# Layer 2 of a fused attention and two-layer kernel: five token tiles in place of six

## The chip, the cores and the metric

The kernel runs on one core of one Trainium2 chip. The time is that of the device for one execution, in microseconds (us); the median of three runs is quoted. PE is TensorE (PEld its weight loads), DVE is VectorE, ACT is ScalarE, POOL is GpSimd, and SP is the engine that issues nearly all of the DMAs.

## The reference, cut to what matters

Attention over q, k and v of 4 batches, 8 heads, 576 positions and 64 elements a head (heads 0 to 3 look back 32 positions, heads 4 to 7 at every 32nd position before), and then two layers on 2304 tokens of width 512, with 2048 hidden columns in each.

```python
scores = np.where(masks[None, :, :, :], scale * np.matmul(q, k.transpose(0, 1, 3, 2)), -1000000000.0)
attn = np.exp(scores - np.max(scores, axis=-1, keepdims=True))
attn_out = np.matmul(attn / (np.sum(attn, axis=-1, keepdims=True) + 1e-09), v)
x = attn_out.transpose(0, 2, 1, 3).reshape(B * S, H * D)
h = np.maximum(x @ w_in, 0.0)
x = h * h @ w_out                                     # layer 1
h = x @ w_in2
g = np.maximum(h, 0.0) + alpha * np.minimum(h, 0.0)
return g @ w_out2                                     # layer 2
```

## The kernel before

The tokens are ordered so that layer 1 runs over seven tiles: three of 256 tokens (the first three blocks of 64 of every batch) and four of 384. `COLS` and `OFFS` hold their widths and starts. Layer 2 runs over six tiles of 384 tokens (`NTILE = 6`, `T` = 384).

The program is a list of steps. A step is one tile and one of 16 blocks `f` of 128 hidden columns. `emit_h` multiplies the block's 128 columns of `w_in` with the tile's x, on PE, into the PSUM bank `ps_h`: 4 chunks of the width 512, and 3 matmuls a chunk, since every operand is held as a high part and a low part (`xh`, `xl`, and the two halves of a weight slot `w{f}`) and three of the four products are taken. That is 12 matmuls, each over all the columns of the tile. `emit_g` applies the activation: for layer 2 two ACT instructions out of PSUM (`g` and `u`), one on DVE that joins them with alpha, and one ACT copy that makes the high part `gh`; `emit_gl` makes the low part `gl` on DVE one step later. `emit_y` multiplies with `w_out` into the PSUM banks `ps_y0` to `ps_y3`. In layer 1 the output is kept with its 512 columns on the partitions: 4 banks, 12 matmuls over the columns of the tile. In layer 2 the tokens are on the partitions: one bank for 128 tokens (`NSUB` = 3 of them in a tile), 3 matmuls a bank, each over 512 columns of `w_out`. On PE a step n therefore reads: the h part of step n+1, then the y part of step n, first the products with `gh` and then those with `gl`. After the last block of a tile `evac` copies the banks to SBUF and stores them: of layer 1 into a buffer `y1` in DRAM, of layer 2 into the output. `load_x2` and `split_x2` fetch layer 2's x from `y1` and split it.

Layer 1's x is written by the attention part, in buffers that `x_tile` hands out. The strided heads (class `Strided`) are worked out on DVE alone: keys and values are loaded by `load_kv` into the pool tag `kv`, and read by `score_mul` (L450) and `value_mul` (L491). The weights arrive as raw 64-bit words (`load_w`, L148, two DMAs of 512 KB for a block) and are turned into high and low parts by `convert_a` to `convert_d`, on ACT (L159, L162, L185) and DVE (L171, L172, L175, L191), between the other work: those of layer 1 during the first two tiles, those of layer 2 during the last tile of layer 1 and the first of layer 2.

The order on SP is the order in which the code issues (`manual_schedule`); so is ACT's from step 48 on. PE, DVE and, before step 48, ACT are ordered by the scheduler of the tile framework. A DMA on SP that waits for a buffer holds back all DMAs behind it.

Of the kernel before, what the change touches and what calls it, by code (L numbers as in the profile page):

```python
# [7 lines left out]
F32 = mybir.dt.float32  # L8
F32R = mybir.dt.float32r
# [7 lines left out]
P = 128  # L17
D = 64
# [1 line left out]
NEG = -1.0e30  # L20
EPS = 1e-9
SCALE = 1.0 / float(D) ** 0.5
NTILE = 6


TILES = [[(b, i) for b in range(4)] for i in range(3)] + [[(b, i) for i in range(3, 9)] for b in range(4)]
COLS = [D * len(blocks) for blocks in TILES]
OFFS = [sum(COLS[:t]) for t in range(len(TILES))]
# [42 lines left out]
def attn_moe_moe2(  # L71
# [37 lines left out]
    nc = tc.nc  # L109
    NT, DM = out.shape  # L110
    NF = w_in1.shape[0]
    NC = DM // P
    T = NT // NTILE
    NSUB = T // P

    cpool = ctx.enter_context(tc.tile_pool(name="const", bufs=1))
    wpool = ctx.enter_context(tc.tile_pool(name="w", bufs=1))
# [79 lines left out]

    def x_tile(t):
        if t not in x_sb:
            kw = {"bufs": 1} if t == 2 else {}  # L200
            x_sb[t] = tuple(
                xpool.tile([P, NC, COLS[t]], F32R, tag=nm[:2] if t != 2 else nm, name=f"{nm}{t}", **kw)
                for nm in ("xh_c", "xl_c")
            )
        return x_sb[t]


# [196 lines left out]
    class Strided:  # L404
# [15 lines left out]
        def load_kv(self, kind):  # L420

            b, e = self.b0, self.b0 + self.nb
            if kind == "k":
                t = spool.tile([P, self.nb, self.a1, D], F32, tag="kv", name="kv", bufs=3)
                src = ks[b:e, :, 0:self.a1, :].rearrange("b p a d -> p b a d")
            else:
                t = spool.tile([P, self.nb, D, self.a1], F32, tag="kv", name="kv", bufs=3)
                src = (vs1 if self.t == 2 else vs)[b:e].rearrange("b p d a -> p b d a")
            nc.sync.dma_start(out=t, in_=src)
            setattr(self, kind, t)  # L430
# [117 lines left out]
    steps = [(0, t, f) for t, f in FIRST]  # L548
    steps += [(0, t, f) for t in range(2, NL1) for f in range(NF)]
    SECOND = len(steps)  # L550
    steps += [(1, t, f) for t in range(NTILE) for f in range(NF)]
    g_sb, y_ps, ybank, hs = {}, {}, {}, {}
    x2, x2raw, y1 = {}, {}, {}

    def cols_of(n):
        return COLS[steps[n][1]] if n < SECOND else T

    def emit_h(n):
        l, t, f = steps[n]
# [11 lines left out]
    def emit_g(n):  # L571
        l, t, f = steps[n]
        m = cols_of(n)
        h = hs.pop(n)[:, 0:m]
        g = gpool.tile([P, T], F32, tag="g", name="g")[:, 0:m]
        gh = gpool.tile([P, T], F32R, tag="gh", name="gh")[:, 0:m]
        if l == 0:
            nc.scalar.activation(out=g, in_=h, func=AF.Relu)  # L578
            nc.scalar.activation(out=gh, in_=g, func=AF.Square)  # L579
            nc.scalar.activation(out=g, in_=g, func=AF.Square)  # L580
        else:
            u = spool.tile([P, T], F32, tag="pr", name="u", bufs=2)
# [16 lines left out]
    def emit_y(n):  # L599
        l, t, f = steps[n]  # L600
        gh, gl = g_sb.pop(n)
        w = wslot[l, f]
        no = NC if l == 0 else NSUB
        if f == 0:
            for o in range(no):
                if (l, t) != (0, 1):
                    ybank[o] = psum(f"y{o}")
                first = COLS[0] if (l, t) == (0, 1) else 0
                y_ps[l, t, o] = ybank[o][:, first:first + (cols_of(n) if l == 0 else DM)]
        order = [(part, o) for part in range(2) for o in range(no)]  # L610
# [15 lines left out]

    def evac(t, layer):
        no = NC if layer == 0 else NSUB
        cols = COLS[t] if layer == 0 else DM
        if layer == 0:  # L630
            y1[t] = dpool.tile([P, NC, cols], F32, tag=f"y1_{t}", name=f"y1_{t}")
        tags = (("so", 2, 1), ("wt", 2, 2)) if layer == 0 else (("so", 1, 1), ("sq", 1, 1), ("wt", 1, 2))
        if layer == 0 and t < 2:
            tags = (("wt", 2, 2),) * 2
        evs = []
        for tag, per, bufs in tags:
            ev = spool.tile([P, per, cols], F32, tag=tag, name="ev", bufs=bufs)
            evs += [ev[:, i, :] for i in range(per)]
        for o in range(no):
            ev = evs[o]  # L640
            y = y_ps.pop((layer, t, o))
            if layer == 1 and t == NTILE - 1 and o > 0:

                rows, half = slice(t * T + o * P, t * T + (o + 1) * P), DM // 2
                nc.vector.tensor_copy(ev[:, 0:half], y[:, 0:half])
                nc.sync.dma_start(out=out[rows, 0:half], in_=ev[:, 0:half])
                nc.scalar.activation(out=ev[:, half:], in_=y[:, half:], func=AF.Copy)
                nc.scalar.dma_start(out=out[rows, half:], in_=ev[:, half:])
                continue
# [89 lines left out]
    def plan():  # L739
        at(loads, 2 * NF, load_alpha)  # L740
        at(fill, 2 * NF + 4, negate_alpha)
        for t in range(2, NL1):
            base = (t - 1) * NF if t > 2 else 0
            for j, (u, p) in enumerate([(u, p) for u in range(2) for p in range(2)]):
                put_unit(base + UNITS_AT.get(t, (0, 3, 6, 9))[j], Unit(t, p, u), 3)
            first, last = STRIDED_AT.get(t, (0, 14))
            put_strided(base + first, base + last, t)
        put_kv_loads()
        for f in range(len(EARLY), NF):
            if f >= len(LOAD_AFTER):  # L750
# [213 lines left out]
```

## Time and profile before

| | |
|---|---|
| median of three runs | 889.06 us |
| the three runs | 888.34, 889.06, 896.01 us |
| the profiled execution, first to last instruction (its span) | 887.5 us |
| the profiled execution's own time | not recorded apart from its span |
| PE busy, share of the span | 866.4 us, 98% |
| DVE, ACT busy | 554.1 us, 453.0 us |

The median lies 1.6 us above the span: that is taken for what lies around the span. A busy share is a mean over stages: DVE is busy 62% of the whole, in layer 2 much less, in the first tiles nearly all the time. PE's matmuls overlap, so that a row's length is longer than the distance to the next; the distance between the starts of two rows is what a matmul costs.

### The profile page before, as it was taken

To read this page: it belongs to the slowest core of one execution; us is meant where nothing else is said; L and a number is where in the kernel's file an instruction comes from. 1 tells how busy PE (TensorE), PEld (TensorE's weight loads), DVE (VectorE), ACT (ScalarE), POOL (GpSimd) and SP (SyncE) were. 2 spreads that over 40 slices of the span, in tenths; PEclk is the share of its full clock that TensorE was granted. 3 is DMA by queue.
4 is the path that set the end of the run, shared out by engine and by line. 5 is a ranking of instruction groups with operands and counts; after the bars stand their busy time and mean duration, and the time that the engine had idled before them with its cause. 6 is when DMAs were issued, how large, how long until landed. Compare 5 with 4: busy or idle time off the path is not lost.

```text
span 887.5 us, 13794 instructions
## 1 busy us (share of the span) xinstructions
PE 866.4 (98%) x5448; PEld 814.4 (92%) x5448; DVE 554.1 (62%) x878; ACT 453.0 (51%) x1064; POOL 1.5 (0%) x10
## 2 busy tenths in 40 slices
PE   6799999999999999999999999999999999999997
PEld 5689999999999999999999999999999998999996
DVE  5899999996869788793687983233233233233222
ACT  5789756555445545454676663344344334334333
POOL 0000000000000000000000000000000000000000
PEclk9999999999999999999999999999999999999999
DMA  9990304221012212101777101001001001000001
GB/s 285 381 357 14 125 11 113 62 92 55 23 52 75 72 52 74 49 8 46 269 277 248 55 10 55 9 10 50 13 10 44 20 10 37 27 9 35 2 1 37
DMA packets 33825, 70.34 MB, mean 79 GB/s; under 512 B 5728, under 2 KB 18144, under 8 KB 33760
## 3 DMA queue, kind: packets, MB, share of 16 engines
q1 hardware_dynamic: 33472, 69.20, 23.0%
q8 instruction: 43, 0.70, 0.3%
q10 hardware_dynamic: 288, 0.26, 0.1%
q14 instruction: 22, 0.18, 0.1%
HBM read 60.01 MB, written 9.44 MB: 78 GB/s over the span
## 4 chain that ended last, share of the span: by engine, by line
PE 92%; DMA 5%; ACT 2%; DVE 1%; issue 0%; SPq 0%; ACTq 0%; DVEq 0%
PE ps_h L566 44%; PE ps_y L622 44%; DMA wraw<-in_w1o_dram 2%; DMA att_w<-in_q_dram 2%; PE ps_s L245 1%; PE ps_o L299 1%; DMA wraw<-in_w1i_dram 1%; PE ps_pt L289 1%; ACT wraw L159 0%; ACT att_w L267 0%; DVE g L585 0%; ACT ev L651 0%; DVE w L191 0%; DVE wt L172 0%; ACT wraw L162 0%
## 5 line engine op out<-in xcount | busy, mean ns | idle before, releaser
L566 PE MATMUL ps_h<-xh_c,w 128*128 128x384 f32 (+1 forms) x896 | 220.3, 314 | 3.2 <-DVE w L191 1.3
L566 PE MATMUL ps_h<-xh,w 128*128 128x384 f32 x768 | 212.5, 337 | 0.2 <-ACT u L584 0.2
L585 DVE SCALAR_TENSOR_TENSOR g<-u,nalpha,g 128x384 f32<-128x384 f32 x96 | 59.3, 618 | 192.1 <-ACT u L584 192.1
L594 DVE TENSOR_TENSOR gl<-g,gh 128x384 fp32r<-128x384 f32 (+1 forms) x208 | 109.2, 525 | 102.5 <-ACT g L580 52.4
L566 PEld LDWEIGHTS ps_h<-xh_c,w 128*128 128x128 f32 x896 | 156.9, 189 | 4.9 <-ACT w L185 1.6
L622 PE MATMUL ps_y<-gh,w 128*128 128x384 f32 (+1 forms) x896 | 158.3, 318 | 1.4 <-ACT gh L579 1.4
L622 PE MATMUL ps_y<-w,gh 128*128 128x512 f32 x576 | 149.3, 394 | 0.1
L566 PEld LDWEIGHTS ps_h<-xh,w 128*128 128x128 f32 x768 | 140.4, 188 | 4.8 <-ACT u L584 0.6
L622 PEld LDWEIGHTS ps_y<-gh,w 128*128 128x128 f32 x896 | 137.9, 189 | 2.8 <-ACT gh L579 1.6
L566 PE MATMUL ps_h<-xl_c,w 128*128 128x384 f32 (+1 forms) x448 | 139.9, 312 | 0.0
L583 ACT ACTIVATE g<-ps_h 128x384 f32<-128x384 f32 x96 | 47.2, 492 | 165.3 <-PE ps_h L566 165.2
L566 PE MATMUL ps_h<-xl,w 128*128 128x384 f32 x384 | 128.9, 336 | 0.0
L578 ACT ACTIVATE g<-ps_h 128x384 f32<-128x384 f32 (+1 forms) x112 | 49.6, 443 | 143.3 <-PE ps_h L566 141.8
L622 PEld LDWEIGHTS ps_y<-w,gh 128*128 128x128 f32 x576 | 106.5, 188 | 17.3 <-ACT gh L588 0.6
L588 ACT ACTIVATE gh<-g 128x384 fp32r<-128x384 f32 x96 | 50.5, 526 | 72.5 <-DVE g L585 72.5
L622 PE MATMUL ps_y<-gl,w 128*128 128x384 f32 (+1 forms) x448 | 86.1, 313 | 0.0
L566 PEld LDWEIGHTS ps_h<-xl_c,w 128*128 128x128 f32 x448 | 84.8, 189 | 0.1
L622 PE MATMUL ps_y<-w,gl 128*128 128x512 f32 x288 | 82.3, 392 | 0.0
L566 PEld LDWEIGHTS ps_h<-xl,w 128*128 128x128 f32 x384 | 72.1, 188 | 4.0
L622 PEld LDWEIGHTS ps_y<-gl,w 128*128 128x128 f32 x448 | 71.8, 189 | 0.4
L622 PEld LDWEIGHTS ps_y<-w,gl 128*128 128x128 f32 x288 | 54.1, 188 | 12.6
L580 ACT ACTIVATE g<-g 128x384 f32<-128x384 f32 (+1 forms) x112 | 53.6, 479 | 2.8
(100 smaller groups left out, 842.0 us busy)
## 6 DMA issues: line engine op xcount, KB each, us to landing
wraw<-in_w1i_dram SPq DMA_DIRECT2D x16, 512.0 KB, 8.9
wraw<-in_w1o_dram SPq DMA_DIRECT2D x16, 512.0 KB, 9.1
wraw<-in_w2i_dram SPq DMA_DIRECT2D x16, 512.0 KB, 3.7
wraw<-in_w2o_dram SPq DMA_DIRECT2D x16, 512.0 KB, 4.7
qk<-in_qk_dram SPq DMA_DIRECT2D x16, 336.0 KB, 3.9
out_dram<-ev SPq DMA_DIRECT2D x16, 256.0 KB, 2.3
y<-ev SPq DMA_DIRECT2D x16, 192.0 KB, 2.1
x2raw<-y SPq DMA_DIRECT2D x16, 192.0 KB, 3.2
```

Source lines behind the costliest of these rows:

```text
L245: nc.tensor.matmul(s, self.qk[:, j, 0:P], self.qk[:, j, P:], start=True, stop=True)
L289: nc.tensor.transpose(self.pt_ps[0:96, P * j:P * j + P], self.e[:, j, :], ident)
L299: nc.tensor.matmul(self.o[64 * h:64 * h + 64, 64 * j:64 * j + 64], self.v[:, j, D * h:D * h + D], self.pt[:, P * j + 64 * h:P * j + 64 * h ...
L566: nc.tensor.matmul(h[:, 0:b.shape[2]], a, b[:, c, :], start=(c == 0 and i == 0), stop=(c == NC - 1 and i == 2))
L578: nc.scalar.activation(out=g, in_=h, func=AF.Relu)
L580: nc.scalar.activation(out=g, in_=g, func=AF.Square)
L583: nc.scalar.activation(out=g, in_=h, func=AF.Relu)
L585: nc.vector.scalar_tensor_tensor(out=g, in0=u, scalar=nalpha[:, f:f + 1], in1=g, op0=ALU.mult, op1=ALU.add)
L588: nc.scalar.activation(out=gh, in_=g, func=AF.Copy)
L594: nc.vector.tensor_tensor(out=gl, in0=g, in1=gh.bitcast(F32), op=ALU.subtract)
L622: nc.tensor.matmul(y, a, b, start=(f == 0 and i == 0 and (l, t) != (0, 1)), stop=(f == NF - 1 and i == 2), skip_group_check=(l == 0 and t ...
```

## The change

Layer 2 runs over five tiles, three of 512 tokens and two of 384 (`WIDTHS`, `STARTS`); its buffers are as wide as the widest. A tile of 512 uses all four y banks, and `evac` has four buffers for it. The first two tiles of layer 1 share one buffer for x, of 512 columns, each its half; the third tile of layer 1 (256 columns), which had a buffer of its own, now takes the second of the two buffers. The pool tag `kv` has two buffers in place of three, and `put_kv_loads` looks two uses back.

```diff
-NTILE = 6
+WIDTHS = (512, 512, 512, 384, 384)
+STARTS = [sum(WIDTHS[:t]) for t in range(len(WIDTHS))]
...
-    T = NT // NTILE
-    NSUB = T // P
+    T = max(WIDTHS)
+    assert sum(WIDTHS) == NT
...
-            kw = {"bufs": 1} if t == 2 else {}
-            x_sb[t] = tuple(
-                xpool.tile([P, NC, COLS[t]], F32R, tag=nm[:2] if t != 2 else nm, name=f"{nm}{t}", **kw)
+            ts = (0, 1) if t < 2 else (t,)
+            whole = [
+                xpool.tile([P, NC, sum(COLS[u] for u in ts)], F32R, tag=nm[:2], name=f"{nm}{t}")
                 for nm in ("xh_c", "xl_c")
-            )
+            ]
+            for u in ts:
+                a = OFFS[u] - OFFS[ts[0]]
+                x_sb[u] = tuple(x[:, :, a:a + COLS[u]] for x in whole)
...
-                t = spool.tile([P, self.nb, self.a1, D], F32, tag="kv", name="kv", bufs=3)
+                t = spool.tile([P, self.nb, self.a1, D], F32, tag="kv", name="kv", bufs=2)
...
-        no = NC if l == 0 else NSUB
+        no = NC if l == 0 else WIDTHS[t] // P
...
-        tags = (("so", 2, 1), ("wt", 2, 2)) if layer == 0 else (("so", 1, 1), ("sq", 1, 1), ("wt", 1, 2))
+        tags = (("so", 2, 1), ("wt", 2, 2)) if layer == 0 else (("so", 1, 1), ("sq", 1, 1), ("wt", 1, 2), ("wt", 1, 2))
...
-        r = spool.tile([P, T], F32, tag="kv", name="x2raw", bufs=3)
+        r = spool.tile([P, T], F32, tag="kv", name="x2raw", bufs=2)[:, 0:WIDTHS[t]]
...
-            if i >= 3:
-                n = max(n, kv_uses[i - 3][0][1] + 1)
+            if i >= 2:
+                n = max(n, kv_uses[i - 2][0][1] + 1)
```

The change adds five lines to the file, so that a line of the changed kernel lies one to five lower than before.

The first place is the first step of layer 2. PE before, from the y part of the first block to the first of the next h part (`w1_0` is layer 2's block 0, `xh2_0` the x of its first tile):

```order
L622 MATMUL ps_y0_5623<-w1_0_5122,gh_5563 128x512 [waits Activation_49]
L622 MATMUL ps_y0_5623<-w1_0_5122,gh_5563 128x512
L622 MATMUL ps_y1_5624<-w1_0_5122,gh_5563 128x512 [waits Activation_49]
L622 MATMUL ps_y1_5624<-w1_0_5122,gh_5563 128x512
L622 MATMUL ps_y2_5625<-w1_0_5122,gh_5563 128x512 [waits Activation_49]
L622 MATMUL ps_y2_5625<-w1_0_5122,gh_5563 128x512
L622 MATMUL ps_y0_5623<-w1_0_5122,gl_5595 128x512 [waits DVE_49]
L622 MATMUL ps_y1_5624<-w1_0_5122,gl_5595 128x512
L622 MATMUL ps_y2_5625<-w1_0_5122,gl_5595 128x512
L566 MATMUL ps_h_5639<-xh2_0_5206,w1_2_5250 128x384 [waits Activation_49]
```

PE now:

```order
L626 MATMUL ps_y0_5621<-w1_0_5120,gh_5561 128x512 [waits Activation_49]
L626 MATMUL ps_y0_5621<-w1_0_5120,gh_5561 128x512
L626 MATMUL ps_y1_5622<-w1_0_5120,gh_5561 128x512 [waits Activation_49]
L626 MATMUL ps_y1_5622<-w1_0_5120,gh_5561 128x512
L626 MATMUL ps_y2_5623<-w1_0_5120,gh_5561 128x512 [waits Activation_49]
L626 MATMUL ps_y2_5623<-w1_0_5120,gh_5561 128x512
L626 MATMUL ps_y3_5624<-w1_0_5120,gh_5561 128x512 [waits Activation_49]
L626 MATMUL ps_y3_5624<-w1_0_5120,gh_5561 128x512
L626 MATMUL ps_y0_5621<-w1_0_5120,gl_5593 128x512 [waits DVE_49]
L626 MATMUL ps_y1_5622<-w1_0_5120,gl_5593 128x512
L626 MATMUL ps_y2_5623<-w1_0_5120,gl_5593 128x512
L626 MATMUL ps_y3_5624<-w1_0_5120,gl_5593 128x512
```

A fourth bank is added to the y part, and the matmuls of the h part (the row behind these) go over 512 columns in place of 384. DVE at the same place, before (`wraw_5499` and `wraw_5540` are the raw weights of blocks 13 and 14, `wt_5612` the work buffer of block 8):

```order
L171 TENSOR_SCALAR wraw_5499<-wraw_5499 128x1024 [waits DMAHW1_49,DMAHW0_49]
L585 SCALAR_TENSOR_TENSOR g_5562<-u_5564,nalpha_80,g_5562 128x384 [waits DVE_49,Activation_49]
L594 TENSOR_TENSOR gl_5595<-g_5562,gh_5563 128x384 [waits PE_49,Activation_49]
L172 SCALAR_TENSOR_TENSOR wt_5612<-wraw_5286 128x1024
L171 TENSOR_SCALAR wraw_5540<-wraw_5540 128x1024 [waits DMAHW3_49,DMAHW2_49]
L175 SCALAR_TENSOR_TENSOR wt_5612<-wraw_5286,wt_5612 128x1024 [waits DVE_49]
L585 SCALAR_TENSOR_TENSOR g_5616<-u_5618,nalpha_80,g_5616 128x384 [waits Activation_49]
```

DVE now:

```order
L172 TENSOR_SCALAR wraw_5497<-wraw_5497 128x1024 [waits DMAHW1_49,DMAHW0_49]
L589 SCALAR_TENSOR_TENSOR g_5560<-u_5562,nalpha_80,g_5560 128x512 [waits DVE_49,Activation_49]
L172 TENSOR_SCALAR wraw_5538<-wraw_5538 128x1024 [waits DMAHW3_49,DMAHW2_49,PE_49]
L598 TENSOR_TENSOR gl_5593<-g_5560,gh_5561 128x512 [waits Activation_49]
L173 SCALAR_TENSOR_TENSOR wt_5610<-wraw_5284 128x1024
L176 SCALAR_TENSOR_TENSOR wt_5610<-wraw_5284,wt_5610 128x1024 [waits DVE_49]
L589 SCALAR_TENSOR_TENSOR g_5614<-u_5616,nalpha_80,g_5614 128x512 [waits Activation_49]
```

The first instruction on the weights of block 14, which waits for their DMA, has moved ahead of the `gl` of layer 2's first step.

The second place is in the first two tiles. The queue of SP before (`kv_961` and `kv_1191` are the keys and the values of the second strided group, `wraw_1193` the weights of layer 1's block 14):

```order
L429 DMA kv_961<-in_ks_dram 128x2x384 [waits DMAHW0_49]
L415 DMA sq_1000<-in_qs_dram 128x2x128 [waits DMAHW1_49,DVE_49]
L148 DMA wraw_1002<-in_w1i_dram 128x1024 [waits DMAHW2_49]
L148 DMA wraw_1002<-in_w1o_dram 128x1024 [waits DMAHW3_49]
L230 DMA qk_1047<-in_q2_dram 128x448 [waits DMAHW4_49]
L238 DMA v_1049<-in_v2_dram 96x256 [waits DMAHW5_49]
L148 DMA wraw_1096<-in_w1i_dram 128x1024 [waits DMAHW6_49,PE_49,Activation_49]
L148 DMA wraw_1096<-in_w1o_dram 128x1024 [waits DMAHW7_49]
L429 DMA kv_1191<-in_vs1_dram 128x2x384 [waits DMAHW0_49]
L148 DMA wraw_1193<-in_w1i_dram 128x1024 [waits DMAHW1_49]
L148 DMA wraw_1193<-in_w1o_dram 128x1024 [waits DMAHW2_49]
L230 DMA qk_1244<-in_q2_dram 128x448 [waits DMAHW3_49,PE_49]
```

SP now:

```order
L433 DMA kv_959<-in_ks_dram 128x2x384 [waits DMAHW0_49,DVE_49]
L419 DMA sq_998<-in_qs_dram 128x2x128 [waits DMAHW1_49]
L149 DMA wraw_1000<-in_w1i_dram 128x1024 [waits DMAHW2_49]
L149 DMA wraw_1000<-in_w1o_dram 128x1024 [waits DMAHW3_49]
L234 DMA qk_1045<-in_q2_dram 128x448 [waits DMAHW4_49]
L242 DMA v_1047<-in_v2_dram 96x256 [waits DMAHW5_49]
L149 DMA wraw_1094<-in_w1i_dram 128x1024 [waits DMAHW6_49,PE_49,Activation_49]
L149 DMA wraw_1094<-in_w1o_dram 128x1024 [waits DMAHW7_49]
L433 DMA kv_1189<-in_vs1_dram 128x2x384 [waits DMAHW0_49,DVE_49]
L149 DMA wraw_1191<-in_w1i_dram 128x1024 [waits DMAHW1_49]
L149 DMA wraw_1191<-in_w1o_dram 128x1024 [waits DMAHW2_49]
L234 DMA qk_1242<-in_q2_dram 128x448 [waits DMAHW3_49,PE_49]
```

The order is the same. The keys now wait for DVE, as the load of the strided queries right behind them did before for the same reads, and the values wait for DVE too: for its last `value_mul` on the first group's values, whose buffer they take. ACT where the weights of block 14 are first used, before (`g_1077` and `gh_1078` belong to block 6 of the second tile):

```order
L185 ACTIVATE w0_9_1055<-wt_1020 128x2x512 [waits DVE_49]
L159 ACTIVATE wraw_1193<-wraw_1193 128x1024 [waits DMAHW2_49,DMAHW1_49]
L267 ACTIVATE e_1031,stat_1032<-e_1031,stat_1032 128x96 [waits DVE_49]
L578 ACTIVATE g_1077<-ps_h_1059 128x256 [waits PE_49]
L267 ACTIVATE e_1031,stat_1032<-e_1031,stat_1032 128x96
L579 ACTIVATE gh_1078<-g_1077 128x256 [waits Activation_49]
L516 ACTIVATE xh_c2_1131<-ot_1072 128x128 [waits DVE_49]
L580 ACTIVATE g_1077<-g_1077 128x256 [waits Activation_49]
L516 ACTIVATE xh_c2_1131<-ot_1074 128x128 [waits DVE_49]
L162 ACTIVATE wraw_1193<-wraw_1193 128x1024
L578 ACTIVATE g_1126<-ps_h_1101 128x256 [waits PE_49]
L579 ACTIVATE gh_1127<-g_1126 128x256 [waits Activation_49]
```

ACT now:

```order
L186 ACTIVATE w0_9_1053<-wt_1018 128x2x512 [waits DVE_49]
L271 ACTIVATE e_1029,stat_1030<-e_1029,stat_1030 128x96 [waits DVE_49]
L271 ACTIVATE e_1029,stat_1030<-e_1029,stat_1030 128x96
L520 ACTIVATE xh_c2_1129<-ot_1070 128x128 [waits DVE_49]
L520 ACTIVATE xh_c2_1129<-ot_1072 128x128 [waits DVE_49]
L582 ACTIVATE g_1075<-ps_h_1057 128x256 [waits PE_49]
L160 ACTIVATE wraw_1191<-wraw_1191 128x1024 [waits DMAHW2_49,DMAHW1_49]
L583 ACTIVATE gh_1076<-g_1075 128x256 [waits Activation_49]
L163 ACTIVATE wraw_1191<-wraw_1191 128x1024
L584 ACTIVATE g_1075<-g_1075 128x256 [waits Activation_49]
L582 ACTIVATE g_1124<-ps_h_1099 128x256 [waits PE_49]
L583 ACTIVATE gh_1125<-g_1124 128x256 [waits Activation_49]
```

The first instruction on block 14's weights, which waits for their two DMAs, now stands behind `g` and ahead of `gh` of block 6.

## Rows read from the trace of the kernel before

**Rows 1.** The page: busy tenths and granted clock in 40 slices; chain by engine.

```profile
PE   6799999999999999999999999999999999999997
...
PEclk9999999999999999999999999999999999999999
...
PE 92%; DMA 5%; ACT 2%; DVE 1%; issue 0%; SPq 0%; ACTq 0%; DVEq 0%
```

**Rows 2.** Busy time by stretch: us, PE, PEld, DVE, ACT, POOL, clock, DMA share.

```profile
640.00:720.00 80.00, 80.00 (x403) 72.45 (x402) 25.31 (x44) 30.09 (x66) 0.00 (x0) 1.00 0.07 23
```

**Rows 3.** Timeline of PE, layer 1, 256 columns: start us, us, what.

```profile
137.11 1.12 PE L622 MATMUL ps_y<-gh,w 128*128 128x256 f32 x8
...
138.55 0.28 PE L566 MATMUL ps_h<-xh_c,w 128*128 128x256 f32 x1
```

**Rows 4.** Timeline of PE, layer 1, 384 columns.

```profile
335.63 1.55 PE L622 MATMUL ps_y<-gh,w 128*128 128x384 f32 x8
...
337.71 0.33 PE L566 MATMUL ps_h<-xh_c,w 128*128 128x384 f32 x1
```

**Rows 5.** Timeline of one step of layer 2.

```profile
700.07 0.33 PE L566 MATMUL ps_h<-xh,w 128*128 128x384 f32 x1
...
702.18 1.55 PE L622 MATMUL ps_y<-w,gh 128*128 128x512 f32 x6
...
704.00 0.53 ACT L588 ACTIVATE gh<-g 128x384 fp32r<-128x384 f32 x1 [0.69 <-DVE g L585]
...
704.26 0.33 PE L566 MATMUL ps_h<-xh,w 128*128 128x384 f32 x1
...
706.37 1.55 PE L622 MATMUL ps_y<-w,gh 128*128 128x512 f32 x6
```

**Rows 6.** Timeline at the border of two tiles of layer 2.

```profile
549.35 0.33 PE L566 MATMUL ps_h<-xh,w 128*128 128x384 f32 x1
...
549.52 1.07 ACT L651 ACTIVATE ev<-ps_y 128x512 f32<-128x512 f32 x2
...
551.46 1.55 PE L622 MATMUL ps_y<-w,gh 128*128 128x512 f32 x6
```

**Rows 7.** Timeline of the DMA queue of SP: issues.

```profile
58.07 0.43 SPq L429 DMA_DIRECT2D kv<-in_vs_dram  x1
...
59.85 0.33 SPq L148 DMA_DIRECT2D wraw<-in_w1o_dram  x1
```

**Rows 8.** Timeline of DVE: last reads of the first strided values.

```profile
74.51 1.82 DVE L491 TENSOR_TENSOR pr<-kv,ss 128x768 f32<-128x768 f32 x2
```

**Rows 9.** Timeline of ACT: first use of the weights of block 14.

```profile
82.48 1.15 ACT L159 ACTIVATE wraw<-wraw 128x1024 f32<-128x1024 f32 x1
...
83.89 0.36 ACT L578 ACTIVATE g<-ps_h 128x256 f32<-128x256 f32 x1
```

**Rows 10.** Timeline of PE at the same place.

```profile
86.11 1.12 PE L622 MATMUL ps_y<-gh,w 128*128 128x256 f32 x8
```

**Rows 11.** The chain that ended last: start us, us, what.

```profile
23.86 9.23 DMA wraw<-in_w1o_dram
...
93.51 5.01 DMA wraw<-in_w1o_dram
```

**Rows 12.** Timeline from layer 1 into layer 2.

```profile
477.78 0.33 PE L566 MATMUL ps_h<-xh,w 128*128 128x384 f32 x1
...
481.94 0.33 PE L566 MATMUL ps_h<-xh,w 128*128 128x384 f32 x1
...
483.12 0.56 DVE L594 TENSOR_TENSOR gl<-g,gh 128x384 fp32r<-128x384 f32 x1 [0.59 <-ACT gh L588]
...
485.60 0.69 DVE L171 TENSOR_SCALAR wraw<-wraw 128x1024 uint32<-128x1024 uint32 x1 [0.79 <-DMA wraw<-in_w2o_dram]
...
486.44 0.45 PE L566 MATMUL ps_h<-xh,w 128*128 128x384 f32 x1 [0.17 <-ACT u L584]
...
490.76 0.34 PE L566 MATMUL ps_h<-xh,w 128*128 128x384 f32 x1
```

More of the change, by code (lines that the diff above doesn't have):

```diff
@@ L423, in load_kv @@
             if kind == "k":
-                t = spool.tile([P, self.nb, self.a1, D], F32, tag="kv", name="kv", bufs=3)
+                t = spool.tile([P, self.nb, self.a1, D], F32, tag="kv", name="kv", bufs=2)
                 src = ks[b:e, :, 0:self.a1, :].rearrange("b p a d -> p b a d")
             else:
-                t = spool.tile([P, self.nb, D, self.a1], F32, tag="kv", name="kv", bufs=3)
+                t = spool.tile([P, self.nb, D, self.a1], F32, tag="kv", name="kv", bufs=2)
                 src = (vs1 if self.t == 2 else vs)[b:e].rearrange("b p d a -> p b d a")
@@ L550, in attn_moe_moe2 @@
     SECOND = len(steps)
-    steps += [(1, t, f) for t in range(NTILE) for f in range(NF)]
+    steps += [(1, t, f) for t in range(len(WIDTHS)) for f in range(NF)]
     g_sb, y_ps, ybank, hs = {}, {}, {}, {}
@@ L555, in cols_of @@
     def cols_of(n):
-        return COLS[steps[n][1]] if n < SECOND else T
+        return COLS[steps[n][1]] if n < SECOND else WIDTHS[steps[n][1]]
     def emit_h(n):
@@ L581, in emit_g @@
         else:
-            u = spool.tile([P, T], F32, tag="pr", name="u", bufs=2)
+            u = spool.tile([P, T], F32, tag="pr", name="u", bufs=2)[:, 0:m]
             nc.scalar.activation(out=g, in_=h, func=AF.Relu)
@@ L627, in evac @@
     def evac(t, layer):
-        no = NC if layer == 0 else NSUB
+        no = NC if layer == 0 else WIDTHS[t] // P
         cols = COLS[t] if layer == 0 else DM
@@ L641, in evac @@
             y = y_ps.pop((layer, t, o))
-            if layer == 1 and t == NTILE - 1 and o > 0:
-                rows, half = slice(t * T + o * P, t * T + (o + 1) * P), DM // 2
+            if layer == 1 and t == len(WIDTHS) - 1 and o > 0:
+                rows, half = slice(STARTS[t] + o * P, STARTS[t] + (o + 1) * P), DM // 2
                 nc.vector.tensor_copy(ev[:, 0:half], y[:, 0:half])
@@ L653, in evac @@
                 nc.vector.tensor_copy(ev, y)
-            dst = y1[t][:, o, :] if layer == 0 else out[t * T + o * P:t * T + (o + 1) * P, :]
+            dst = y1[t][:, o, :] if layer == 0 else out[STARTS[t] + o * P:STARTS[t] + (o + 1) * P, :]
             nc.sync.dma_start(out=dst, in_=ev)
     def load_x2(t, c):
-        r = spool.tile([P, T], F32, tag="kv", name="x2raw", bufs=3)
+        r = spool.tile([P, T], F32, tag="kv", name="x2raw", bufs=2)[:, 0:WIDTHS[t]]
+        lo, hi = STARTS[t], STARTS[t] + WIDTHS[t]
         for u in range(NL1):
-            a, b = max(T * t, OFFS[u]), min(T * t + T, OFFS[u] + COLS[u])
+            a, b = max(lo, OFFS[u]), min(hi, OFFS[u] + COLS[u])
             if a < b:
-                nc.sync.dma_start(out=r[:, a - T * t:b - T * t], in_=y1[u][:, c, a - OFFS[u]:b - OFFS[u]])
+                nc.sync.dma_start(out=r[:, a - lo:b - lo], in_=y1[u][:, c, a - OFFS[u]:b - OFFS[u]])
         x2raw[t, c] = r
@@ L667, in split_x2 @@
             x2[t] = tuple(
-                xpool.tile([P, NC, T], F32R, tag=nm, name=f"{nm}2_{t}") for nm in ("xh", "xl")
+                xpool.tile([P, NC, T], F32R, tag=nm, name=f"{nm}2_{t}")[:, :, 0:WIDTHS[t]] for nm in ("xh", "xl")
             )
@@ L756, in plan @@
             put_convert(1, f, last + 4 + f * 3 // 2)
-        for t in range(NTILE):
+        for t in range(len(WIDTHS)):
             base = SECOND + (t - 1) * NF
```

## The prediction

> **What bounds the kernel now.** First the page's slices: PE shows a 9 from the third slice to the last but one, and the granted clock is full in all 40 of them; the chain that ended last is PE's own for 92% [rows 1]. Then one window of layer 2: in 80 us PE is busy for 80.00, DVE for 25.31 and ACT for 30.09 [rows 2]. So in layer 2 only what PE executes counts, and DVE and ACT have room for tiles a third wider. Whether PE waits for them in a step is read off its timeline: the `gh` that the y part at 706.37 needs is finished at 704.00 + 0.53 = 704.53, which is 1.84 us early [rows 5]. In the first two tiles and where layer 1 ends this is tighter, so that those two places get a term each.
>
> **How the trace stands to the time.** The profiled execution's span is 887.5 us, the median 889.06; I carry the 1.56 between them over unchanged.
>
> **What a matmul costs.** From the distance between starts: 12 matmuls of 256 columns take 138.55 - 137.11 = 1.44 us, 120 ns each [rows 3]; of 384 columns 337.71 - 335.63 = 2.08, 173.3 ns each [rows 4]. The 128 columns between them cost 53.3 ns, so that a line through both leaves 120 - 106.7 = 13.3 ns that do not depend on the width. In layer 2 the h part takes 702.18 - 700.07 = 2.11, 175.8 ns for each of its 12 matmuls of 384, and the y part 704.26 - 702.18 = 2.08, 231.1 ns for each of its 9 matmuls of 512 [rows 5].
>
> The Trainium skill, "TensorE: Matmul & The Clock Gate", section "Back-to-back issue gap", gives for an isolated matmul on a warm engine its columns at 2.4 GHz and 2.5 ns more (109 ns for 256 columns, 163 for 384, 216 for 512), and says that a stream comes out below that at 512. The trace disagrees, with 120, 173.3 and 231.1. By that page the 192 matmuls that the change saves would save 192 x 2.5 = 0.5 us, an estimate by that page, and the time would be 888.6.
>
> **Term 1, the h parts of layer 2.** 1536 tokens move from four tiles into three. Before, 4 x 16 = 64 steps of 2.11 = 135.0 us. Now 48 steps of 12 matmuls over 512 columns. No h matmul of that width is in the trace; the nearest row is the y part's, also 512 columns, in layer 2, with the same operand type: 231.1. That gives 48 x 12 x 0.2311 = 133.1, a gain of **1.9 us**. Bounds: the line through rows 3 and 4 goes to 226.7 ns at 512, which gives 130.6 and a gain of 4.4; a cost that only scales with the columns, 175.8 x 512 / 384 = 234.4, gives 135.0 and no gain. I take 231.1, since it is a measured width and not an extrapolation.
>
> **Term 2, the y parts of layer 2.** A tile of 512 has 12 y matmuls a step where 384 had 9, all 512 columns wide before and now. 96 x 9 = 864 before, 48 x 12 + 32 x 9 = 864 now: 0.
>
> **Term 3, activations, borders, evictions.** A 512-wide step lasts about 2 x 2.77 = 5.55 us in place of 4.19, and its ACT and DVE work grows by a third as well, so the 1.84 us to spare grow to about 2.4. One border of tiles goes; but the h part at the border takes 551.46 - 549.35 = 2.11, as in mid-tile, and the ACT copies end at 549.52 + 1.07 = 550.59, well ahead of the next y [rows 6]. Nothing is to be had there, and the fourth bank, one more copy on DVE, hides behind the next h part of 2.77. Term: 0. Without that cover a copy would cost some 0.5 each (1.07 for two, the same rows) at three borders.
>
> **Term 4, from layer 1 into layer 2.** Before, the two steps from 481.94 take 4.50 and 4.32 (486.44, 490.76) against 4.19: 0.44 over [rows 12]. On DVE the shift of block 14's weights, which waits for its DMA, now stands ahead of the first `gl`. Its DMA does not depend on the change, so the shift ends as before at 485.60 + 0.69 = 486.29; `gl` takes 0.56 x 512 / 384 = 0.75 and is there at 487.04. PE wants it after the h part of step 0 (2.77 from 477.78), layer 1's last y part (2.08), the next h part (2.77) and 8 y matmuls on `gh` (1.85): 487.25. So it is hidden, by only 0.2. Below, the 0.44 that is lost now could go (-0.4), since DVE and ACT have longer steps; above, the shift's DMA could come 1 us later (+0.8). I take **0**, as the two clocks read from the rows say.
>
> **Term 5, values with two buffers.** In the first strided group's place the values were issued at 58.07 and block 14's two weight DMAs behind them by 59.85 [rows 7]. Now the values take the buffer of the first group's values, whose last reads end at 74.51 + 1.82 = 76.33 [rows 8]. So SP stands there some 18 us, and the weights behind it wait with it. If they follow as closely as before (1.8 behind), they are issued by 78.1. A 512 KB weight DMA took 5.01 on a quiet queue, 9.23 in the crowded start [rows 11]; behind a stalled SP little else is under way at 78 us, so I take 5.01 and a landing at 83.1. ACT reaches the first instruction on these weights at 82.48 before; now it stands behind `g`, which ends at 83.89 + 0.36 = 84.25 [rows 9]. Queued behind it on ACT is `gh` of block 6, on which PE's y part at 86.11 waits [rows 10]: the convert instruction takes 1.15 and `gh` about 0.4, as `g` of the same shape, so PE stalls if the weights land later than 84.55. They land 1.4 earlier: **0**, with the cover being those 1.4 us. If the 393 KB of values delay them by their share, 393/1024 x 5.0 = 1.9, the landing is 85.0 and the stall 0.5. With 9.23 and 1.9 it is 89.2 and the stall 4.7, the upper bound. Below nothing there is no room: PE does not wait for anything that these loads now bring earlier. The keys wait too, but for the same reads as the queries' load right behind them did already: 0. The later groups' loads wait for reads of the group before, which ends a good part of a tile ahead of the loads' places: 0.
>
> **Term 6, x and the order on PE.** The shared buffer of tiles 0 and 1 holds the same bytes at other addresses; tile 2 gets a buffer that is free from the start, and tile 3 waits for tiles 0 and 1, which PE left long before. At block 6 of the second tile the `gl` products move behind the next h matmuls: same work, 0.
>
> **Sum.** -1.9 + 0 + 0 + 0 + 0 + 0. Span 885.6, time 885.6 + 1.6 = **887.2 us**.
>
> **The rivals.**
> - *The whole fixed part comes back* (884.7): h matmuls of 512 columns run at the line's 226.7. For it speaks that the line is exact at 256 and 384 in layer 1; against it that 512 columns in layer 2's y part cost 231.1 and even 384 columns cost 2.5 ns more there than in layer 1. Chance 0.20.
> - *No gain* (889.1): cost goes with the columns, so that fewer and wider matmuls do the same work in the same time. 175.8 against 173.3 shows that layer 2 has an extra cost the line does not have, and it may grow with the width. The Trainium skill's fixed part, above, would land next to this. Chance 0.15. This is also the case in which the change doesn't do what it is made of.
> - *Slower, by block 14's weights* (891.9): the landing comes at 89.2 in place of 83.1, ACT waits in its queue ahead of `gh`, and PE waits for `gh`. It decides from a landing 1.9 us later than 84.55, at 86.5, where the stall eats the gain. For it speaks that all DMAs that SP holds back are let go in one go; against it that the data ahead of the weights is little. Chance 0.07.
>
> **How the numbers follow.** The forecast has 0.55, the rivals 0.20, 0.15 and 0.07, anything else 0.03. From 884.6 to 889.6 lie the forecast, the first two rivals and the bounds of terms 1 and 4 with half a microsecond of stall; the slower rival's full price and surprises are left out, 0.10. One per cent is 8.9 us, about what a measurement of this kernel can tell from no change; the bounds together reach from -4.8 to +5.5 and so stay inside it. What is left for a surprise beyond is 0.02 faster and 0.03 slower, and 0.95 for the same.
>
> **What would show it right or wrong.** In layer 2's wide tiles an h part should take 2.77 us (2.72 for the first rival, 2.81 for the second), and a step about 5.55; the steps of the 384 tiles stay at 4.19. SP should stand from about 58 to 76.4 and issue values and block 14's weights in a row; ACT's first instruction on these should show no wait for a DMA of more than a microsecond, and PE no idle time at 84 to 90 us. At the end of layer 1 `gl` should be done by about 487, and PE go on without idle time. Wrong would make it: a y part of 12 matmuls that costs more than 12 x 0.231; a wait for weights that grows from block 14 to 15 and delays the strided work behind it; or a stall of DVE in the first tiles that the order does not show.

## The result, and the profile after

| | before | changed |
|---|---|---|
| median | 888.7 us (4 runs) | 880.98 us (4 runs) |
| lowest run | 887.98 | 880.37 |
| span of the profiled execution | 887.5 | 879.5 |

The ratio is 0.9889, 95% interval 0.9844 to 0.9933; measured once more beside other kernels it was 0.9902 (0.987 to 0.9934). Both intervals lie below 1. By the medians the change gains 7.7 us where 1.9 were forecast, and the time lies below the range.

By place, from the timelines of the two profiled executions: layer 2's first h matmul moved from 477.78 [rows 12] to 477.65, so that everything up to there gave 0.1 (in all eight traces that have a layer 2 this start lies between 476.74 and 477.78). From there to the last h part it took 875.91 - 477.78 = 398.1 before and 868.71 - 477.65 = 391.1 now: **7.1 us, all in layer 2**. After it 0.7 are left, in the landing of the last stores, which varies between executions (from the start of the last matmul to the end 5.1 us before, 4.4 now, 4.2 to 4.7 in the other runs below whose last tile has 384 tokens).

TensorE still bounds. The window of layer 2 that answers to [rows 2], with the same fields:

```profile
640.00:720.00 80.00, 80.00 (x355) 66.27 (x354) 24.12 (x35) 27.76 (x51) 0.00 (x0) 1.00 0.07 24
```

355 matmuls in 80 us where there were 403, with DVE and ACT as idle as before and the same clock. The timeline of one step of a 512 tile answers to [rows 5]:

```profile
599.52 1.98 PE L626 MATMUL ps_y<-w,gh 128*128 128x512 f32 x8
601.34 1.07 PE L626 MATMUL ps_y<-w,gl 128*128 128x512 f32 x4
601.69 0.63 ACT L592 ACTIVATE gh<-g 128x512 fp32r<-128x512 f32 x1 [0.82 <-DVE g L589]
602.24 0.39 PE L570 MATMUL ps_h<-xh,w 128*128 128x512 f32 x1
...
604.96 1.29 PE L626 MATMUL ps_y<-w,gh 128*128 128x512 f32 x5
```

The y part takes 602.24 - 599.52 = 2.72 us, the h part 604.96 - 602.24 = 2.72: 226.7 ns for each of the 24 matmuls. The y part's matmuls, which the change leaves at 512 columns each, cost 231.1 before; they became faster too. The step is 5.44 us, not 5.55. `gh` is there at 602.32, 2.64 us ahead of the y part that needs it.

Now the same timeline where the last 512 tile meets the first of 384:

```profile
735.52 1.98 PE L626 MATMUL ps_y<-w,gh 128*128 128x512 f32 x8
...
738.24 0.33 PE L570 MATMUL ps_h<-xh,w 128*128 128x384 f32 x1
...
740.35 2.01 PE L626 MATMUL ps_y<-w,gh 128*128 128x512 f32 x8
...
743.11 0.33 PE L570 MATMUL ps_h<-xh,w 128*128 128x384 f32 x1
...
745.22 1.55 PE L626 MATMUL ps_y<-w,gh 128*128 128x512 f32 x6
...
747.29 0.33 PE L570 MATMUL ps_h<-xh,w 128*128 128x384 f32 x1
```

At 735.52, after h parts of 512, twelve y matmuls take 2.72. At 740.35, after an h part of 384, the same twelve take 2.76, and the h parts of 384 take 2.11, as in all of layer 2 before. In the two narrow tiles the step stays at 4.19. So by these rows the 231.1 of [rows 5] does not belong to 512 columns as such, but to a stream in which 384 and 512 stand in turn.

The place where layer 1 goes over into layer 2, which answers to [rows 12], shows it a third time:

```profile
477.65 0.39 PE L570 MATMUL ps_h<-xh,w 128*128 128x512 f32 x1
...
480.42 1.57 PE L626 MATMUL ps_y<-gh,w 128*128 128x384 f32 x8
...
482.52 0.39 PE L570 MATMUL ps_h<-xh,w 128*128 128x512 f32 x1
...
483.07 0.69 DVE L172 TENSOR_SCALAR wraw<-wraw 128x1024 uint32<-128x1024 uint32 x1 [0.58 <-DMA wraw<-in_w2o_dram]
...
483.68 0.68 DVE L598 TENSOR_TENSOR gl<-g,gh 128x512 fp32r<-128x512 f32 x1
...
485.28 1.98 PE L626 MATMUL ps_y<-w,gh 128*128 128x512 f32 x8
...
488.00 0.39 PE L570 MATMUL ps_h<-xh,w 128*128 128x512 f32 x1
```

Layer 1's last y part, 12 matmuls of 384, takes 482.52 - 480.42 = 2.10 between two h parts of 512, where it took 2.08 all through layer 1 [rows 4]; the h parts on its two sides take 2.77 and 2.76, the next part of 512 takes 2.72. The DMA of block 14 landed in time for 483.07, not for 485.60 as in the execution before, and `gl` was there at 484.36, 2.7 us ahead of the products that need it (the prediction had 487.04 and 0.2).

In the first tiles, SP's queue, which answers to [rows 7]:

```profile
57.58 0.67 SPq L149 DMA_DIRECT2D wraw<-in_w1o_dram  x1
76.47 0.38 SPq L433 DMA_DIRECT2D kv<-in_vs_dram  x1
...
77.40 0.43 SPq L149 DMA_DIRECT2D wraw<-in_w1o_dram  x1
```

and ACT and PE at the place of [rows 9, 10]:

```profile
83.97 1.16 ACT L160 ACTIVATE wraw<-wraw 128x1024 f32<-128x1024 f32 x1
85.01 0.40 ACT L583 ACTIVATE gh<-g 128x256 fp32r<-128x256 f32 x1
```

```profile
86.22 1.13 PE L626 MATMUL ps_y<-gh,w 128*128 128x256 f32 x8
```

SP stood until 76.47 for the read on DVE; the second half of block 14's weights was issued 0.93 us behind the values, and the weights were there when ACT came to them at 83.97: its row has no wait in brackets. PE goes on at 86.22, against 86.11, and between 40 and 110 us it waits three times in both executions, 2.1, 1.3 and 0.8 us.

### The profile page after: what moved, and what is told of

Same layout as the page of the kernel before. It is cut to its first block, busy times and chain, and to the rows that moved or that the text cites. A ratio compares the mean times of both kernels' runs of the same rounds, so it can differ in the third digit from the quotient of the medians.

```text
span 879.5 us, 13290 instructions
## 1 busy us (share of the span) xinstructions
PE 859.4 (98%) x5256; PEld 788.3 (90%) x5256; DVE 550.1 (63%) x844; ACT 445.2 (51%) x1010; POOL 1.5 (0%) x10
## 4 chain that ended last, share of the span: by engine, by line
PE 93%; DMA 5%; ACT 1%; DVE 0%; SPq 0%; issue 0%; ACTq 0%
PE ps_y L626 45%; PE ps_h L570 45%; DMA wraw<-in_w1o_dram 2%; DMA att_w<-in_qd_dram 1%; PE ps_s L249 1%; PE ps_o L303 1%; DMA att_w<-in_v_dram 1%; PE ps_pt L293 1%; DVE w L192 0%; DVE wt L173 0%; ACT wraw L160 0%; ACT w L186 0%; SPq L234 0%; ACT ev L651 0%; DVE g L589 0%
## 5 line engine op out<-in xcount | busy, mean ns | idle before, releaser
L570 PE MATMUL ps_h<-xh,w 128*128 128x512 f32 (+1 forms) x640 | 197.0, 369 | 0.0
L589 DVE SCALAR_TENSOR_TENSOR g<-u,nalpha,g 128x512 f32<-128x512 f32 (+1 forms) x80 | 55.8, 698 | 190.8 <-ACT u L588 190.8
L598 DVE TENSOR_TENSOR gl<-g,gh 128x384 fp32r<-128x384 f32 (+2 forms) x192 | 106.7, 556 | 101.6 <-ACT g L584 51.8
L626 PE MATMUL ps_y<-w,gh 128*128 128x512 f32 x576 | 144.9, 391 | 0.1
L570 PEld LDWEIGHTS ps_h<-xh,w 128*128 128x128 f32 x640 | 119.0, 188 | 16.2
L587 ACT ACTIVATE g<-ps_h 128x512 f32<-128x512 f32 (+1 forms) x80 | 44.5, 556 | 175.7 <-PE ps_h L570 175.7
L570 PE MATMUL ps_h<-xl,w 128*128 128x512 f32 (+1 forms) x320 | 117.8, 368 | 0.0
L592 ACT ACTIVATE gh<-g 128x512 fp32r<-128x512 f32 (+1 forms) x80 | 47.2, 590 | 63.1 <-DVE g L589 63.1
L626 PE MATMUL ps_y<-w,gl 128*128 128x512 f32 x288 | 79.0, 391 | 0.0
L570 PEld LDWEIGHTS ps_h<-xl,w 128*128 128x128 f32 x320 | 60.1, 188 | 8.9
```

The source lines that it names most:

```text
L570: nc.tensor.matmul(h[:, 0:b.shape[2]], a, b[:, c, :], start=(c == 0 and i == 0), stop=(c == NC - 1 and i == 2))
L589: nc.vector.scalar_tensor_tensor(out=g, in0=u, scalar=nalpha[:, f:f + 1], in1=g, op0=ALU.mult, op1=ALU.add)
L598: nc.vector.tensor_tensor(out=gl, in0=g, in1=gh.bitcast(F32), op=ALU.subtract)
L626: nc.tensor.matmul(y, a, b, start=(f == 0 and i == 0 and (l, t) != (0, 1)), stop=(f == NF - 1 and i == 2), skip_group_check=(l == 0 and t ...
```

## The experiments

The theory formed on these rows: **a change of width costs**. A stream of matmuls of one width takes 13.3 ns and its columns at 2.4 GHz for each (120, 173.3, 226.7 ns at 256, 384, 512 columns; "the line" below). Where parts of 384 and of 512 columns stand in turn, 26 ns more are lost in the 384 part (2.106 us against 2.080) and 41 in the 512 part of nine matmuls (2.081 against 2.040), 66 a pair. Rivals: a y part of nine matmuls on three banks is slow in itself; ScalarE's and VectorE's work beside it slows TensorE; part of the gain comes from the buffers.

### Matmuls alone

A kernel with no attention, no layers and no other engine at work beside TensorE (VectorE and ScalarE are busy for 0.00 us from 20 to 300 us): only stages of matmuls on loaded data, with a weight load for each as in the kernel. Three of its eleven stages:

```python
...
for s in range(12):
    one_bank(12, 384, s)      # 12 matmuls of 384 columns into one bank
    banks(3, 512)             # 9 of 512, on three banks
for s in range(6):
    one_bank(12, 384, s)
    one_bank(12, 384, s + 1)
    banks(3, 512)
    banks(3, 512)
for s in range(8):
    one_bank(12, 512, s)
    banks(3, 512)
...
```

> A kernel of TensorE matmuls alone (it leaves out the whole computation; no activation, no VectorE work beside them), in stages: parts of 12 matmuls of 384 columns; parts of 12 of 512; 12 of 384 and 9 of 512 in turn, as in a step of a narrow layer-2 tile; the same with every part doubled (24 of 384, 18 of 512); 12 of 512 with 9 and with 12 of 512; 12 of 512 with 12 of 384; 12 of 256 with 6 of 512; 12 of 256 with 12 of 384; single matmuls of 384 and 512 in turn; 12 of 384 with 12 of 384. Theory, a change of width costs: 173.3 and 226.7 ns a matmul in every stage of one width, 9 matmuls of 512 on three banks with 12 of 512 too (4.76 us a step); 4.187 us for 12 of 384 with 9 of 512 (4.12 and 0.066); 8.31 for the doubled parts (8.24 and 0.066, since there are as many changes); more than 400 ns for a pair of single matmuls. Rival, three banks and nine matmuls cost: 4.187 in the plain stage, 8.37 in the doubled one, and 9 of 512 take 2.08 beside 12 of 512 too. Rival, ScalarE and VectorE at work beside TensorE cost: 4.12 and 8.24, no stage above its columns.

Its timeline of PE, in these three stages and in a last one of 384 columns alone (`ps_a` is the part that stands for h, `ps_b` for y):

```profile
58.60 2.27 PE L85 MATMUL ps_a<-x,w 128*128 128x384 f32 x12
60.71 2.24 PE L85 MATMUL ps_b<-x,w 128*128 128x512 f32 x9
62.79 2.27 PE L85 MATMUL ps_a<-x,w 128*128 128x384 f32 x12
...
108.84 4.28 PE L85 MATMUL ps_b<-x,w 128*128 128x512 f32 x18
112.96 4.35 PE L85 MATMUL ps_a<-x,w 128*128 128x384 f32 x24
117.15 4.28 PE L85 MATMUL ps_b<-x,w 128*128 128x512 f32 x18
...
157.22 2.20 PE L85 MATMUL ps_b<-x,w 128*128 128x512 f32 x9
159.26 2.88 PE L85 MATMUL ps_a<-x,w 128*128 128x512 f32 x12
161.98 2.20 PE L85 MATMUL ps_b<-x,w 128*128 128x512 f32 x9
...
398.62 2.24 PE L85 MATMUL ps_a<-x,w 128*128 128x384 f32 x12
...
406.94 2.24 PE L85 MATMUL ps_a<-x,w 128*128 128x384 f32 x12
```

The narrow step of the kernel comes out again with nothing else running: 60.71 - 58.60 = 2.11 and 62.79 - 60.71 = 2.08, so ScalarE and VectorE are not the cause. Four parts of 384 columns without a change take 406.94 - 398.62 = 8.32, 173.3 ns a matmul. With doubled parts 24 matmuls of 384 take 117.15 - 112.96 = 4.19 (4.16 by the line) and 18 of 512 take 4.12 (4.08): together 8.31, as the theory said, and not the 8.37 of the rival: the same two losses, though twice the matmuls. Where in a part they lie is seen from the starts of the single matmuls in the same trace:

```profile
110.92 2.20 PE L85 MATMUL ps_b<-x,w 128*128 128x512 f32 x9
...
114.03 3.28 PE L85 MATMUL ps_a<-x,w 128*128 128x384 f32 x18
```

In the part of 18 the first 9 matmuls of 512 take 110.92 - 108.84 = 2.08 us, the last 9 take 112.96 - 110.92 = 2.04, on the line. In the part of 24 the first 6 of 384 take 114.03 - 112.96 = 1.07 (1.04 by the line), the other 18 take 117.15 - 114.03 = 3.12, on the line. Nine matmuls on three banks take 159.26 - 157.22 = 2.04 between parts of 512: 226.7 each. The rival of three banks falls. Other pairs in this kernel: 12 of 512 with 12 of 384 lose 67 ns, as with nine; 12 of 256 with 6 of 512 lose only 20 ns a pair of parts (1.43 and 1.39 us against 1.44 and 1.36), 12 of 256 with 12 of 384 lose nothing (1.43 and 2.09 against 1.44 and 2.08), and single matmuls of 384 and 512 in turn take 413 ns a pair, 13 over the line. The last is more than 400, as expected, and far less than 66 over it: the loss of a change is not paid at once.

### Six tiles of 384 again, with the other edits

```diff
-WIDTHS = (512, 512, 512, 384, 384)
+WIDTHS = (384,) * 6
```

> The changed kernel with six tiles of 384 in layer 2 again; x shared by the first two tiles and two buffers for keys and values stay. Theory, the gain lies in the widths alone (7.1 us in layer 2's steady steps): 888.7, within 0.5 of before, steps of 4.187 throughout layer 2. Rival, the buffers give part of it (earlier conversion of weights, a shorter way from layer 1 into layer 2): 886 to 888, with layer 2 starting earlier.

888.43 us against 888.48 for the kernel before, ratio 1.0001 (0.9977 to 1.0024). The shared x and the two buffers for keys and values show no gain and no loss, within the interval of about 2 us to either side. Its timeline of PE in layer 2 has the old parts again:

```profile
483.09 1.55 PE L626 MATMUL ps_y<-w,gh 128*128 128x512 f32 x6
...
485.17 0.33 PE L570 MATMUL ps_h<-xh,w 128*128 128x384 f32 x1
...
487.28 1.09 PE L626 MATMUL ps_y<-w,gh 128*128 128x512 f32 x4
```

2.08 and 2.11. The 0.44 us that the way into layer 2 lost before [rows 12] is not there with these tiles either: in the execution before, the second halves of blocks 13 and 14 took 7.1 and 7.25 us from issue to the DVE instruction that waited for them (the median landing of layer 2's second halves is 4.7 us in that execution), here DVE did not wait. So the tiles' widths are not the cause; a slow landing in the one profiled execution fits, but there is only one trace of each kernel. Layer 2, first h part to last, takes 397.68 here against 391.05 with the change: 6.6 us are the widths'.

### Half as many changes of width, the same matmuls

Six tiles of 384; from the second one on, two h parts and then two y parts stand together, the h parts in two banks. From there on the order on PE is that of the code, no longer the scheduler's.

```diff
-        h = psum("h")
+        h = psum("s" if n >= PAIRS and n % 2 else "h")
...
+    def run_pairs(ns):
+        for n in ns:
...
+            emit_h(n + 1)
+            if n + 2 < len(steps):
+                emit_h(n + 2)
+            emit_g(n + 1)
+            emit_gl(n + 1)
+            emit_y(n)
+            if n + 2 < len(steps):
+                emit_g(n + 2)
+            emit_y(n + 1)
...
```

> As the run with six tiles of 384, but from layer 2's second tile on two h parts stand together and then two y parts, so that TensorE changes its width half as often; each matmul is the same. Theory, a change of width costs: 80 steps save half of 0.066 us, 2.6 us less than with six tiles of 384: 886.1. Rival, nine matmuls over three banks cost 41 ns a y part and 384 columns in layer 2 cost 26 ns an h part, wherever they stand: no difference, 888.7. Rival, ScalarE and VectorE at work beside TensorE cost it: no difference either, as the work beside it is the same.

884.76 us, ratio to the kernel before 0.9952 (0.9934 to 0.997): 3.7 less than with single parts by the medians. From layer 2's first h part to its last it took 397.68 with single parts and 395.08 with pairs, 2.60 less, where 80 x 0.033 = 2.6 was expected; the rest of the medians' difference is not in layer 2, and ten of the twelve runs of the kernel with single parts spread from 887.05 to 889.86, the other two stand at 894.3 and 894.8. The timeline of PE shows how:

```profile
701.92 1.55 PE L627 MATMUL ps_y<-w,gh 128*128 128x512 f32 x6
...
704.00 1.52 PE L627 MATMUL ps_y<-w,gh 128*128 128x512 f32 x6
...
706.04 0.33 PE L571 MATMUL ps_s<-xh,w 128*128 128x384 f32 x1
...
708.15 0.33 PE L571 MATMUL ps_h<-xh,w 128*128 128x384 f32 x1
...
710.23 1.55 PE L627 MATMUL ps_y<-w,gh 128*128 128x512 f32 x6
```

The first y part after a change takes 2.08, the second 706.04 - 704.00 = 2.04; the first h part 2.11, the second 2.08. The first of each pair pays, the second is on the line. Both rivals, which said "no difference", fall.

### Four tiles of 512 and one of 256

```diff
-WIDTHS = (512, 512, 512, 384, 384)
+WIDTHS = (512, 512, 512, 512, 256)
```

> The changed kernel with four tiles of 512 and one of 256 in layer 2. Columns and matmuls are as many as in the changed kernel, so that by a fixed part and the columns alone the time is the same, 881.0, less about 0.7 for a shorter last step. Theory, a change of width costs: 16 steps with changes in place of 32 save 1.06 us if a change from 512 to 256 costs as much as one to 384 (879.2), and nothing if it costs twice that (880.3). Rival, nine matmuls on three banks cost: the 256 tile has six on two banks, a y part of 6 x 231 = 1.39 and h parts of 1.44; 878.9.

879.16 us, ratio 0.9901 (0.9874 to 0.9928), by the medians 1.7 to 1.8 less than the changed kernel's 880.87 and 880.98, though the intervals of the ratios (the changed kernel's were 0.9889 and 0.9902) do not tell the two apart. Its timeline of PE in the 256 tile:

```profile
839.06 1.09 PE L626 MATMUL ps_y<-w,gh 128*128 128x512 f32 x4
...
840.45 0.28 PE L570 MATMUL ps_h<-xh,w 128*128 128x256 f32 x1
...
841.88 1.09 PE L626 MATMUL ps_y<-w,gh 128*128 128x512 f32 x4
```

1.39 and 1.43 against 1.36 and 1.44 by the line, as in the matmuls alone: 20 ns a step where 384 loses 66. So 32 x 0.066 - 16 x 0.020 = 1.8 us should be the gain over the changed kernel. From the first h part of layer 2 to the end the changed kernel takes 401.9 in both its traces, this one 399.9: 2.0, which leaves 0.2 for the shorter last step. The time came out as the theory said, 879.2, but by luck: that sum had 1.06 for the changes and 0.7 for the last step, and both were off.

### The pairs in the changed kernel and in the last one

The same edit in the changed kernel's two tiles of 384, and in the 256 tile of the kernel with four tiles of 512; with the changed kernel beside them on the same chip.

> The changed kernel with two h parts and then two y parts together in its two tiles of 384, so that 32 steps have half as many changes of width. Theory, a change of width costs 0.066 us a pair of changes: 32 x 0.033 = 1.06 us less than the changed kernel, 879.9. Rival, the narrow step costs what it costs: 881.0.

> The changed kernel once more, beside the others on one chip: 881.0, as before.

> Four tiles of 512 and one of 256, and in the 256 tile two h parts and two y parts together. Theory, with the 20 ns a step that the matmuls alone showed for 256 with 512: 16 x 0.010 = 0.16 us less than with four tiles of 512 and one of 256 (879.16), which is not measurable: 879.0. Rival, a change to 256 costs as much as one to 384: 878.6.

880.54, 880.87 and 878.86 us; the ratios to the kernel before are 0.991 (0.9883 to 0.9938), 0.9902 (0.987 to 0.9934) and 0.9888 (0.9849 to 0.9927). In the traces the pairs shorten layer 2, first h part to last, from 391.05 to 390.05 (1.00, expected 1.06) and from 391.29 to 391.15 (0.14, expected 0.16). In the medians the first shows 0.3 only and isn't resolved; in its trace 0.6 of the 1.00 are left at the end (from the first h part to the end 401.9 and 401.3). The lowest medians are those of four tiles of 512 and one of 256 with or without pairs, 878.9 to 879.2. They beat the kernel before; over the changed kernel the medians and the traces (399.8 and 399.9 against 401.9 twice) show about 2 us, which the intervals of the ratios do not resolve.

### How long the loss lasts, and other widths

Matmuls alone again, with parts of other lengths and widths; the part of its code with the lengths (`mm` is one matmul, here of 512 columns):

```python
...
for n in (2, 4, 6, 9, 15, 24):
    for s in range(144 // n):
        one_bank(n, 384, s)
        for k in range(n):
            mm(wide[s % 4], k, 512, k == 0, k == n - 1)
...
```

> TensorE matmuls alone again (the whole computation is left out): 12 of 128, 320, 448 and 480 columns with 12 of 512 in turn; 12 of 384 with 12 of 448; and 384 with 512 in parts of 2, 4, 6, 9, 15 and 24 matmuls. Theory, each change starts a loss that is spread over the next 15 or so matmuls and is then over: with parts of 9, 15 and 24 a pair of parts loses 66 ns, with shorter ones less (13 at parts of 1). Rival, the loss is paid at once at the change: 66 ns for every length of parts. On the widths: if the loss goes with the difference of widths, 128 loses most and 480 least; since 256 lost only 20 ns and 384 lost 66, I expect instead that 320 and 448 lie near 66 and 128 near nothing.

The timeline of PE for parts of 6, 9 and 15:

```profile
340.74 1.21 PE L85 MATMUL ps_a<-x,w 128*128 128x384 f32 x6
341.78 1.55 PE L85 MATMUL ps_b<-x,w 128*128 128x512 f32 x6
343.17 1.21 PE L85 MATMUL ps_a<-x,w 128*128 128x384 f32 x6
...
399.14 1.73 PE L85 MATMUL ps_a<-x,w 128*128 128x384 f32 x9
400.70 2.24 PE L85 MATMUL ps_b<-x,w 128*128 128x512 f32 x9
402.78 1.40 PE L85 MATMUL ps_a<-x,w 128*128 128x384 f32 x7
...
457.78 2.79 PE L85 MATMUL ps_a<-x,w 128*128 128x384 f32 x15
460.41 3.60 PE L85 MATMUL ps_b<-x,w 128*128 128x512 f32 x15
463.85 2.44 PE L85 MATMUL ps_a<-x,w 128*128 128x384 f32 x13
```

A pair of parts of 15 takes 463.85 - 457.78 = 6.07, against 15 x 0.400 = 6.00; of 9, the first pair, behind parts of 6, takes 402.78 - 399.14 = 3.64 against 3.60, and the median of the 16 pairs is 3.667 (67 ns over); of 6, 343.17 - 340.74 = 2.43 against 2.40 (34 over); of 4, 20 over, of 2, 26 over, and of 24, 66 over. From 9 on the loss is whole and grows no more, below that it is smaller, though parts of 2 lose more than parts of 4: it is spread over several matmuls behind a change (fewer than the 15 or so expected) and not paid at once. On the widths the expectation was mostly wrong. Parts of 12 beside 12 of 512 lose 21 ns a pair with 320 columns (not 66), 47 with 448, 40 with 480, and 12 of 384 beside 12 of 448 lose 80. These four are against the line drawn through other widths: no stage had 320, 448 or 480 columns alone. With 128 columns, where next to nothing was expected, a pair takes 1.29 + 2.83 = 4.12 us, 0.60 over the line. There the matmuls of 128 and their weight loads start some 112 ns apart in the trace, in step with each other, where the line has 66.7; whether the loads set the pace there was not tested. The loss does not simply go with the difference of widths.

## Why the prediction was wrong

*The bound and the method* were right: TensorE alone sets layer 2, before and after, and the distance between starts is what counts. *Terms 3, 5 and 6* were right too. `gh` came 2.64 us early (about 2.4 forecast); the kernel with all the edits but the widths shows no difference; SP stood to 76.47 (forecast 76.4), and the weights came in time, with `gh` at 85.41 before PE's 86.22.

*Term 2 is the step that failed*: "96 x 9 = 864 before, 48 x 12 + 32 x 9 = 864 now: 0" counts y matmuls and holds their cost at 231.1. Their number is the same, their cost is not: in the 512 tiles it is 226.7. That is 48 x 12 x 0.0044 = 2.6 us.

*Term 1 was mis-sized* by the same fault. It took 231.1 for an h matmul of 512 columns, since that was "a measured width and not an extrapolation", and forecast 1.9; measured are 226.7 and 64 x 2.106 - 48 x 2.720 = 4.2. The first rival had this number right, by the line through 120 and 173.3, and stood at 0.20. What spoke for it, that the line "is exact at 256 and 384 in layer 1", was no evidence, since the line was drawn through these two; the matmuls alone at 512 columns are what confirms it. With it came what no rival said, that the y parts follow. The Trainium skill, "TensorE: Matmul & The Clock Gate", section "Back-to-back issue gap", gives 2.5 ns beside the columns for an isolated matmul. The matmuls alone, in parts of one width, show 13.3 at 384 and at 512, so that for these matmuls the measurement decides against it.

Put the other way round, the 6.8 us of layer 2's steady steps are 192 matmuls less at 13.3 ns = 2.6, and 64 steps without a change of width at 0.066 = 4.2. The remaining 0.3 of the 7.1 is what the execution before lost on the way into layer 2 (0.44), less a few changes of width at the borders.

What could have been seen from the rows alone: [rows 4] and [rows 5] gave an excess of 2.5 ns on 384 columns in layer 2 and of 4.4 on 512, over the line drawn through layer 1's two widths. The prediction saw both, and put the first down to layer 2 and the second to 512 columns. One thing that the two parts share and layer 1 lacks is that they stand beside each other with two widths, and that the change takes away. A rival "both excesses go" would have cost one line: 48 x 24 x 0.2267 against 64 x 4.187, 261.1 against 268.0, and 882.2.

*Term 4's transition*: the way into layer 2 lost 0.44 before and next to nothing now, inside its bounds (-0.4 to +0.8). The runs tie it to when DMAs landed in the profiled execution, not to longer steps of DVE and ACT, the reason that the bound was given for. The term took that landing over from one execution to the next ("the shift ends as before"); it came 2.5 us earlier, so that the 0.2 us of cover became 2.7, and that nothing was lost there is in part luck.

*The range*: the prediction says that 884.6 to 889.6 holds the bounds of terms 1 and 4 with half a microsecond of stall. By its own terms these reach from 889.1 - 4.4 - 0.4 = 884.3 to 889.1 + 0.8 + 0.5 = 890.4. The miss does not hang on it.

What stays open is why a change of width costs TensorE this much, and which pairs of widths cost: the runs show where in a part it is lost, and how much for some pairs, but no rule behind it.

## What to carry to other kernels

Fit a line through matmul costs in a stretch with one width, and ask of every excess elsewhere what the rows with it share, before it is booked as a price of a shape. A term "the same number of instructions, so 0" holds only if their neighbours stay the same too. Where a matmul-bound loop alternates two widths, try equal widths, or fewer and longer parts of each, and time the pair alone: it took one small kernel of matmuls to tell.

## What the runs showed of the hardware that was not expected

On this chip, with weights of 128 columns loaded for each matmul and the clock at its upper level (2.4 GHz), matmuls of one width start 173.3 ns apart at 384 columns and 226.7 at 512, on three banks as on four. Parts of 384 and 512 in turn lose 66 ns a pair, 26 in the first six matmuls of the 384 part and 41 in the first nine of the 512 part, whether the parts have 9, 12, 15 or 24 matmuls, and less in shorter ones (34 at 6, 20 at 4, 26 at 2). The pair of 256 with 512 loses 20, of 256 with 384 nothing, and of 384 with 448, against the line, 80.
